# Linear attention and two MLPs in one kernel: the softmax of k on turned tiles, and a new order of the work

## The chip, the cores and the metric

The kernel runs on one core of a Trainium2 chip. The metric is the device time of one execution in microseconds. Engines are named as the profile names them: PE is TensorE (matmuls), PEld its weight loads, DVE is VectorE, ACT is ScalarE, POOL is GpSimd, SP is SyncE, which here issues the DMAs.

## What is computed

```python
def _attn_ref(q, k, v):                       # q, k, v: 4 x 8 x 576 x 64, float32
    q_s = softmax of q along the 64 features
    k_s = np.exp(k - np.max(k, axis=2, keepdims=True))
    k_s = k_s / (np.sum(k_s, axis=2, keepdims=True) + 1e-09)     # along the 576 tokens
    kv = np.einsum('bhsd,bhse->bhde', k_s, v)
    return np.einsum('bhsd,bhde->bhse', q_s, kv)

x = attn_out, as 2304 tokens x 512
x = softplus(x @ w_in) @ w_out                # 512 -> 2048 -> 512
return elu(x @ w2_in) @ w2_out                # 512 -> 2048 -> 512
```

## The kernel before

The 2304 tokens are six blocks of 384 (t = 0 to 5); two blocks make a pair p. For a pair, each of the two MLPs (m = 0, 1) runs through eight quads f of 256 hidden features. All but the first quad use a seven-product scheme on half blocks: the sums that it needs of x and of the weights are formed on ACT and DVE, each as a high and a low part that TensorE multiplies as fp32r. The products are `ub`, `ua`, `uc` (up, line 975) and `acc`, `Pa`, `Pb`, `Pc` (down, lines 1174, 1205, 1347). The first quad (m = p = f = 0) is done directly in fp32: `up` (line 1037) and its `acc` (line 1142).

Before a block of x exists, attention has to be done for it. Heads go in pairs hp = 0 to 3, one head on partitions 0 to 63 and the other on 64 to 127. `add_k` makes the 64 x 64 matrices `kvbd` of a batch b and its head pairs; `add_q` makes x for a block from q and `kvbd`: `pq` (transposes, line 627), `xq` (copy), `px` (line 643), `sx` (copy, line 656). Block 0 needs batch 0, four head pairs one at a time; block 1 needs batches 0 and 1, and batch 1 goes in two calls with two head pairs each. For these two blocks `add_k` has the tokens of a head on 64 partitions, nine to a partition. In `k` the maximum over tokens therefore goes across partitions:

- DVE takes the maximum over the nine (`mt`, `mx`, line 356, four instructions), TensorE transposes it (`pt`, line 364), DVE reduces (`m`, line 368), TensorE spreads the result over the partitions (`pb`, line 376), DVE subtracts it from k (line 383), ACT takes exp (line 391).
- TensorE multiplies by v, to which a column of ones is added (`pk`, line 400: 18 matmuls of 64 x 64 by 65 columns for a head pair, in fp32, with the two heads on different halves of the array). DVE makes the reciprocal of the sums (`rs`, lines 415 and 419), ACT scales into `kvbd` (line 429, two instructions for a head pair).

Later blocks take their k on all 128 partitions (`add_k_wide`); that code is unchanged.

The order of all work comes from a planner in the file (`class Plan`). Each piece is a step with an engine, an estimated duration, what it reads and writes, and which buffer ring it needs. `order()` runs through time and picks on each engine, among steps that can start, the one with the earliest due time; due times run back from those of the `up` and `acc` steps, and the table `PRI` moves groups of steps earlier or later (`k00` is k of block 0 and head pair 0, `i3` the input weights of quad 3). Each engine then executes its list in that order. The set `LIGHT` names weight tiles whose first ACT step (line 791) is done as a `Prelu` while the table of exp is loaded; for those the DVE step in line 804 is left out. Buffers matter in one place: k of batch 1 has a ring of one, so its second call is loaded only after `pk` has read the first.

Of the kernel before, what the change touches and what calls it, by code (L numbers as in the profile page):

```python
# [21 lines left out]
class Plan:  # L22
# [38 lines left out]
    def order(self):  # L61
# [23 lines left out]
        seq, gone = [], set()  # L85
        while len(seq) < n:
# [30 lines left out]
            if eng == PE and t < 25:  # L117
                dur *= PE_EARLY
            if i in gone:
                dur = 0.0  # L120
            if i in self.either and (self.tab[i] or table) == "exp":
                gone.add(self.either[i][0])
                self.light.add(self.either[i][1])
# [26 lines left out]
PE_EARLY = 1.6  # L150
# [7 lines left out]
def t_dve(n, fast=False):  # L158
    return 0.069 + n / (1920 if fast else 960)
# [11 lines left out]
def attention_moe_moe_kernel(  # L171
# [34 lines left out]
    P = 128  # L206
# [87 lines left out]
    def bank(t, rows=False):  # L294

        return "ha" if t > 1 else "acc0" if rows and not t else "acc1"

    def add_k(t, b, hps, behind=()):
# [52 lines left out]
        mt = ("mt", b, hps[0])  # L351

        @step(DVE, sum(t_dve(n * x * D) for x in (4, 2, 1, 1)) + 0.37, r=[kk], make=[(mx, "mx"), (mt, "mt")])
        def _():
            half = new(mt)[:, : 4 * n * D].rearrange("p (g c d) -> p g c d", g=n, d=D)
            top = lambda o, x, y: nc.vector.tensor_tensor(o, x, y, op=ALU.max)
            top(half, kt()[:, :, :4], kt()[:, :, 4:8])
            top(half[:, :, :2], half[:, :, :2], half[:, :, 2:])
            top(half[:, :, 0], half[:, :, 0], half[:, :, 1])
            top(new(mx)[:, : n * D].rearrange("p (g d) -> p g d", g=n), half[:, :, 0], kt()[:, :, 8])  # L360

        @step(PE, 0.11, r=[mx], make=[(pt, bank(t))])
        def _():
            nc.tensor.transpose(new(pt)[: n * D, :P], T[mx][:, : n * D], ident)

        @step(DVE, t_dve(128), r=[pt], make=[(m, "m")])
        def _():
            nc.vector.tensor_reduce(
                new(m)[: n * D], T[pt][: n * D, :P].rearrange("d (h p) -> d h p", h=2), axis=AX.X, op=ALU.max
            )  # L370

        @step(PE, 0.12 * n, r=[m], make=[(pb, bank(t))])
        def _():
            p = new(pb)
            for j in range(2):
                nc.tensor.matmul(
                    p[64 * j : 64 * j + 64, : n * D], T[m][: n * D, j : j + 1].to_broadcast([n * D, 64]),
                    ident[: n * D, : n * D], start=True, stop=True,
                )

        @step(DVE, t_dve(n * C * D), r=[pb], w=[kk])
        def _():
            nc.vector.tensor_tensor(
                kt(), kt(),
                T[pb][:, : n * D].rearrange("p (g o d) -> p g o d", g=n, o=1).to_broadcast([P, n, C, D]),
                op=ALU.subtract,
            )

        @step(ACT, t_act(n * C * D), w=[kk], tab="exp")
        def _():  # L390
            nc.scalar.activation(kt(), kt(), AF.Exp)

        @step(PE, 1.3 * n, r=[kk, vk], make=[(pk, bank(t))])
        def _():
            p = new(pk)
            for g in range(n):
                for c in range(C):
                    for j in range(2):
                        rows = slice(64 * j, 64 * j + 64)
# [7 lines left out]
    def add_kv(b, hps):  # L407
# [13 lines left out]
        eng = ACT  # L421

        @step(eng, 0.65 * n, r=[pk, rs], w=[("kvbd", b % 2, hp) for hp in hps])
        def _():
            for g, hp in enumerate(hps):
                for j in range(2):
                    rows = slice(64 * j, 64 * j + 64)
                    o, i, f = kvbd[b % 2, hp][rows, rows], pkv()[rows, g, :D], T[rs][rows, g : g + 1]
                    nc.scalar.activation(o, i, AF.Copy, scale=f)
# [273 lines left out]
    def add_forms(m, p):  # L703
# [50 lines left out]
        (0, "i", 0), (0, "i", 2), (0, "i", 3), (0, "i", 4), (0, "i", 5), (0, "o", 0), (0, "o", 6), (0, "o", 7),  # L754
        (1, "i", 4), (1, "o", 1), (1, "o", 6), (1, "o", 7),
# [996 lines left out]
```

## Time and profile before

| | |
|---|---|
| median of 3 runs | 817.21 us (816.12 to 818.25) |
| the profiled execution | 817.89 us |
| its span | 815.8 us |
| PE busy | 796.9 us, 98% of the span |
| DVE, ACT busy | 655.2 us, 581.5 us |
| HBM | 154.66 MB read, 56.10 MB written |

The profiled execution is 0.7 us above the median. All windows and start times below count from the start of the span. A matmul in plain fp32 leaves two records in the trace, one in fp32r and a transpose leave one. A duration is that of a record or of a merged run of records; since matmuls are pipelined, the time that a run of them takes is read from its start to the start of what follows.

### The profile page before, as it was taken

The page shows a single profiled execution, that of the slowest core. Times are in us where ns is not written, and L with a number is a line of the kernel's source. Part 1 is how long each engine was busy: PE and PEld are TensorE (multiplying, and loading weights), DVE is VectorE, ACT ScalarE, POOL GpSimd, SP SyncE. Part 2 cuts the span into 40 slices and gives each one's busy share as a digit, 9 for nine tenths or more (in the row PEclk, how much of TensorE's full clock was granted, in tenths as well). Part 3 has the DMA queues.
Part 4 walks back from the last instruction along what each step waited for, and adds up shares of the span by engine and source line. Part 5 has one row for each costly group of instructions (what it writes and reads, how often), then busy time and mean ns, then how long its engine had stood idle before and what let it go on. Part 6 is the DMA issues. An engine that isn't in the chain of part 4 may idle for free.

```text
span 815.8 us, 13597 instructions
## 1 busy us (share of the span) xinstructions
PE 796.9 (98%) x5200; PEld 746.6 (92%) x5200; DVE 655.2 (80%) x1061; ACT 581.5 (71%) x909; POOL 6.9 (1%) x28
## 2 busy tenths in 40 slices
PE   5799999999999999999999999999999999999998
PEld 4578999989899999999999988999999999999998
DVE  7899989989888959987599875579776798767775
ACT  4899898977778879767658765486656675557552
POOL 2000000000000000000000000000000000000000
PEclk9799999999999999999999999999999999999999
DMA  9767797457988557888955889876688767687563
GB/s 284 207 216 224 277 293 223 174 188 270 270 266 301 191 203 271 275 300 290 319 209 215 329 326 358 293 257 261 246 320 297 299 248 252 264 282 301 198 246 134
DMA packets 84993, 211.66 MB, mean 259 GB/s; under 512 B 16064, under 2 KB 51392, under 8 KB 74432
## 3 DMA queue, kind: packets, MB, share of 16 engines
q1 hardware_dynamic: 84928, 210.79, 74.3%
q8 instruction: 41, 0.67, 0.3%
q14 instruction: 24, 0.20, 0.1%
HBM read 154.66 MB, written 56.10 MB: 258 GB/s over the span
## 4 chain that ended last, share of the span: by engine, by line
PE 88%; DMA 4%; ACT 4%; DVE 3%; issue 1%; SPq 0%; ACTq 0%; DVEq 0%
PE acc L1174 23%; PE ub L975 23%; PE uc L975 11%; PE Pb L1347 10%; PE ua L975 6%; PE Pc L1347 5%; PE Pa L1347 3%; PE acc L1205 2%; PE px L643 2%; DMA wos<-wv 1%; DMA q<-in_q_dram 1%; PE pq L627 1%; PE pk L535 1%; DMA wos<-wk 1%; DMA raw_i<-in_moe_w_in_dram 1%
## 5 line engine op out<-in xcount | busy, mean ns | idle before, releaser
L975 PE MATMUL ub<-xf,wf_i 128*128 128x384 f32 x1128 | 229.3, 337 | 1.2 <-ACT s L988 1.2
L975 PEld LDWEIGHTS ub<-xf,wf_i 128*128 128x128 f32 x1128 | 191.4, 188 | 8.5 <-ACT s L988 2.2
L1174 PE MATMUL acc<-gh,wo_o 128*128 128x512 f32 x736 | 160.8, 340 | 0.0
L1174 PEld LDWEIGHTS acc<-gh,wo_o 128*128 128x128 f32 x736 | 118.7, 188 | 11.5
L975 PE MATMUL uc<-xf,wf_i 128*128 128x384 f32 x564 | 114.2, 336 | 0.3 <-DVE xf L728 0.2
L988 ACT COPY s<-ub 128x384 f32<-128x384 f32 x141 | 67.0, 475 | 60.9 <-PE ub L975 59.8
L975 PEld LDWEIGHTS uc<-xf,wf_i 128*128 128x128 f32 x564 | 96.2, 188 | 3.2 <-ACT g L1058 0.5
L1174 PE MATMUL acc<-gl,wo_o 128*128 128x512 f32 x368 | 94.0, 336 | 0.0
L1009 DVE TENSOR_TENSOR h<-uc,s 128x384 f32<-128x384 f32 x94 | 52.1, 554 | 40.2 <-PE uc L975 33.0
L1174 PEld LDWEIGHTS acc<-gl,wo_o 128*128 128x128 f32 x368 | 56.3, 188 | 7.7
L1115 DVE TENSOR_TENSOR gl<-g,gh 128x768 fp32r<-128x768 f32 x54 | 51.4, 953 | 10.5 <-ACT gh L1111 10.3
L975 PE MATMUL ua<-xf,wf_i 128*128 128x384 f32 x282 | 57.2, 337 | 0.0
L975 PEld LDWEIGHTS ua<-xf,wf_i 128*128 128x128 f32 x282 | 48.5, 188 | 1.1 <-DVE h L1009 0.3
L1111 ACT CAST gh<-g 128x768 fp32r<-128x768 f32 x54 | 45.2, 837 | 5.3 <-DVE g L1102 4.5
L1058 ACT ACTIVATE g<-h 128x384 f32<-128x384 f32 (+1 forms) x46 | 31.5, 686 | 7.7 <-DVE h L1009 7.6
L1009 DVE TENSOR_TENSOR h<-ua,s 128x384 f32<-128x384 f32 x47 | 26.0, 553 | 5.9 <-PE ua L975 4.8
L994 ACT COPY h<-ub 128x384 f32<-128x384 f32 x24 | 11.5, 479 | 26.0 <-PE ub L975 25.6
L1205 PE MATMUL acc<-wo_o,gh 128*128 128x512 f32 x96 | 29.9, 392 | 0.0
L890 DVE TENSOR_TENSOR wf_i<-r_i,wf_i 128x1024 fp32r<-128x1024 f32 x20 | 24.4, 1221 | 5.6 <-ACT wf_i L886 5.5
L890 DVE TENSOR_TENSOR wf_i<-st_i,wf_i 128x768 fp32r<-128x768 f32 x27 | 25.6, 950 | 2.0 <-ACT wf_i L886 2.0
L886 ACT CAST wf_i<-r_i 128x1024 fp32r<-128x1024 f32 x20 | 21.0, 1049 | 7.5 <-PE uc L975 5.9
L886 ACT CAST wf_i<-st_i 128x768 fp32r<-128x768 f32 x27 | 22.6, 839 | 4.5 <-DVE st_i L869 4.4
(328 smaller groups left out, 1498.7 us busy)
## 6 DMA issues: line engine op xcount, KB each, us to landing
wf_i<-wfd SPq DMA_DIRECT2D x20, 1792.0 KB, 7.9
ws<-wos SPq DMA_DIRECT2D x35, 1024.0 KB, 6.2
raw_i<-in_moe_w_in_dram SPq DMA_DIRECT2D x32, 512.0 KB, 5.4
raw_o<-in_moe_w_out_dram SPq DMA_DIRECT2D x32, 512.0 KB, 4.7
wo_o<-wod SPq DMA_DIRECT2D x15, 1024.0 KB, 5.5
r_i<-w32i SPq DMA_DIRECT2D x20, 512.0 KB, 4.1
wod<-wo_o SPq DMA_DIRECT2D x8, 1024.0 KB, 5.2
wfd<-wf_i SPq DMA_DIRECT2D x4, 1792.0 KB, 7.1
```

The costliest lines, as they stand in the source:

```text
L643: nc.tensor.matmul(ov[:, :, n0 : n0 + n_], kvbd[b % 2, hp], iv[:, :, n0 : n0 + n_], start=True, stop=True,)
L886: nc.scalar.copy(view(0, lo, n), get())
L890: nc.vector.tensor_tensor(view(1, lo, n), get(), view(0, lo, n).bitcast(F32), op=ALU.subtract)
L975: nc.tensor.matmul(ps[:, :BLK], T[wk][:, lo : lo + P], T[xk][:, (2 * c + kc) * BLK : (2 * c + kc + 1) * BLK], start=(i in first and kc == ...
L988: nc.scalar.copy(new(sk), T[key][:, :BLK])
L1009: nc.vector.tensor_tensor(T[hk][:, half * BLK : (half + 1) * BLK], T[key][:, :BLK], T[sk], op=ALU.add)
L1058: nc.scalar.activation(o, i, AF.Softplus)
L1111: nc.scalar.copy(new(hk), T[gk])
L1115: nc.vector.tensor_tensor(new(lk), T[gk], T[hk].bitcast(F32), op=ALU.subtract)
L1174: nc.tensor.matmul(ps, T[wk][:, lo : lo + P], T[g][:, cols], start=(first and n == 0 and starts), stop=(f == NQ - 1 and j == 1 and n == 2) ...
L1205: nc.tensor.matmul(ps, T[g][:, col : col + P], T[wk][:, (2 * a + j) * DM : (2 * a + j + 1) * DM], start=(first and n == 0), stop=(f == PRE ...
L1347: nc.tensor.matmul(ps[:, x * 256 : x * 256 + 256], T[fk][a][:, r * P : (r + 1) * P], T[ck][:, q * 512 + b * 256 : q * 512 + b * 256 + 256] ...
```

## The change

For blocks 0 and 1 `add_k` turns k of a head pair so that the 64 features of a head stand on partitions and its tokens along the free dimension. Turning is 18 matmuls of 64 x 64 whose moving side is a 64 x 64 identity, in plain fp32, not transposes: `ka`, and `kx` for the last of the nine pieces. DVE reduces the maximum along the free dimension (two instructions and a small one that joins and negates them), ACT takes exp from PSUM with the maximum as its bias (two instructions). The result is turned back in the same way (`ea`, and another slice of `kx`), DVE copies it to `k` in SBUF (two instructions), and `pk` follows as before. `mt`, `mx`, `pt`, `pb` and the subtraction are gone for these blocks. `kx` is one PSUM tile for all head pairs, opened at the start.

`kvbd` of batches 0 and 1 is scaled by DVE instead of ACT. The planner's model of a slow TensorE is another one (a state with a gap and a run in place of "the first 25 us"), `pk` has 1.07 in place of 1.3 us in it and a turning 0.54 us. `LIGHT` has 19 members in place of 12, and `PRI` is new, so that the order changes in all of the first MLP and the start of the second. The last 1305 rows of PE's list are the same.

```diff
-PE_EARLY = 1.6
+PE_EARLY, PE_GAP, PE_RUN = 1.85, 2.0, 4.6
...
+        def turned_to(wide, more, get):
+            for c in range(C):
+                for rows in two:
+                    to = T[wide][rows, c * 64 : c * 64 + 64] if c < C - 1 else T[kx][rows, more * 64 : more * 64 + 64]
+                    nc.tensor.matmul(to, get(rows, c), ident[rows, rows], start=True, stop=True)
...
-        def _():
-            half = new(mt)[:, : 4 * n * D].rearrange("p (g c d) -> p g c d", g=n, d=D)
...
+            @step(PE, 0.54, r=[kk, ("kxr",), *([("kt", 0, hp)] if b else [])], make=[(ka, "ha" if early else "acc1")], w=[k9], hold=[kx])
+                turned_to(ka, hp, lambda rows, c: kt()[rows, g, c, :])
...
+                nc.vector.tensor_reduce(new(m)[:, :1], T[ka], axis=AX.X, op=ALU.max)
+                nc.vector.tensor_reduce(T[m][:, 1:2], last_(0), axis=AX.X, op=ALU.max)
...
+                nc.vector.tensor_scalar(
+                    T[m][:, :1], T[m][:, :1], T[m][:, 1:2], -1.0, op0=ALU.max, op1=ALU.mult
+                )
...
+                nc.scalar.activation(flat()[:, :512], T[ka], AF.Exp, bias=T[m][:, :1])
+                nc.scalar.activation(flat()[:, 512:], last_(0), AF.Exp, bias=T[m][:, :1])
...
+            @step(PE, 0.54, r=[kt_, *([("ke", 0, hp)] if b else [])], make=[(ea, "ha" if early else "acc1")], w=[e9], hold=[kk, kx])
+                turned_to(ea, 4 + hp, lambda rows, c: flat()[rows, c * 64 : c * 64 + 64])
...
+                copy(flat()[:, :512], T[ea])
+                copy(flat()[:, 512:], last_(1))
...
-        @step(PE, 1.3 * n, r=[kk, vk], make=[(pk, bank(t))])
+        @step(PE, 1.07 * n, r=[vk] + [("ke", b, hp) for hp in hps], make=[(pk, bank(t))], hold=[kk])
...
-        eng = ACT
+        eng = DVE if b in (0, 1) else ACT
...
+                        nc.vector.tensor_scalar(o, i, f, None, op0=ALU.mult)
...
-        k00=165, q00=153.5, k01=696.5, q01=214, k02=165.5, q02=417, k03=1898, q03=1032, k10=31.5, q10=133, k12=1338.5,
+        k00=196.5, q00=20, k01=25, q01=221, k02=64, q02=111, k03=94.5, q03=184.5, k10=141, q10=208.5, k12=174, q12=27,
```

The start of PE's list, before (in a name the first number is the batch or block, the second the head pair; `k_1_2` holds head pairs 2 and 3 of batch 1):

```order
L364 MATMUL pt_0_3_205<-ident_147,mx_0_3_200 64x128
L376 MATMUL pb_0_3_218<-ident_147,m_0_3_209 64x64 x2
L364 MATMUL pt_1_2_226<-ident_147,mx_1_2_215 128x128
L376 MATMUL pb_1_2_241<-ident_147,m_1_2_232 64x128 x2
L400 MATMUL pk_0_3_248<-v_0_3_182,k_0_3_183 64x65 x18
L364 MATMUL pt_0_1_284<-ident_147,mx_0_1_239 64x128
L364 MATMUL pt_0_2_291<-ident_147,mx_0_2_278 64x128
L376 MATMUL pb_0_1_298<-ident_147,m_0_1_289 64x64 x2
L400 MATMUL pk_1_2_308<-v_1_2_186,k_1_2_187 64x65 x36
L400 MATMUL pk_0_1_368<-v_0_1_190,k_0_1_191 64x65 x18
```

and now:

```order
L370 MATMUL ka_0_0_198<-ident_147,k_0_0_183 64x64 x16
L370 MATMUL kx_196<-ident_147,k_0_0_183 64x64 x2
L370 MATMUL ka_0_3_229<-ident_147,k_0_3_191 64x64 x16
L370 MATMUL kx_196<-ident_147,k_0_3_191 64x64 x2
L370 MATMUL ea_0_0_250<-ident_147,k_0_0_183 64x64 x16
L370 MATMUL kx_196<-ident_147,k_0_0_183 64x64 x2
L419 MATMUL pk_0_0_283<-v_0_0_182,k_0_0_183 64x65 x18
L370 MATMUL ka_1_3_304<-ident_147,k_1_2_187 64x64 x16
L370 MATMUL kx_196<-ident_147,k_1_2_187 64x64 x2
L370 MATMUL ea_0_3_331<-ident_147,k_0_3_191 64x64 x16
L370 MATMUL kx_196<-ident_147,k_0_3_191 64x64 x2
L370 MATMUL ka_0_2_359<-ident_147,k_0_2_194 64x64 x16
```

Each head pair had one transpose, two spreading matmuls and its `pk`; now it has two turnings of 18 matmuls ahead of `pk`, and head pair 0 of batch 0 is the first.

The place of the first `up` in PE's list, before:

```order
L627 MATMUL pq_0_1_568<-ident_147,q_0_1_272 128x128 x3
L627 MATMUL pq_0_0_573<-ident_147,q_0_0_387 128x128 x3
L376 MATMUL pb_1_0_581<-ident_147,m_1_0_577 64x128 x2
L643 MATMUL px_0_1_587<-xq_0_1_567,kvbd0_1_149 128x384
L643 MATMUL px_0_0_590<-xq_0_0_572,kvbd0_0_148 128x384
L1037 MATMUL up_0_0_0_604<-sx_0_0_179,w_ti_0_i_0_543 128x384 x4
L627 MATMUL pq_1_0_621<-ident_147,qn_1_0_609 128x128 x3
L627 MATMUL pq_1_1_628<-ident_147,qn_1_0_609 128x128 x3
L400 MATMUL pk_1_0_634<-v_1_0_395,k_1_0_396 64x65 x36
L1037 MATMUL up_0_0_1_676<-sx_0_0_179,w_ti_0_i_0_543 128x384 x4
```

and now, from the last `px` of block 0:

```order
L665 MATMUL px_0_0_753<-xq_0_0_740,kvbd0_0_148 128x384
L649 MATMUL pq_1_2_759<-ident_147,qn_1_2_751 128x128 x3
L370 MATMUL ka_1_0_767<-ident_147,k_1_0_691 64x64 x16
L370 MATMUL kx_196<-ident_147,k_1_0_691 64x64 x2
L370 MATMUL ka_1_1_792<-ident_147,k_1_0_691 64x64 x16
L370 MATMUL kx_196<-ident_147,k_1_0_691 64x64 x2
L649 MATMUL pq_1_3_812<-ident_147,qn_1_2_751 128x128 x3
L1060 MATMUL up_0_0_0_824<-sx_0_0_180,w_ti_0_i_0_503 128x384 x4
L370 MATMUL ea_1_0_841<-ident_147,k_1_0_691 64x64 x16
L370 MATMUL kx_196<-ident_147,k_1_0_691 64x64 x2
L665 MATMUL px_1_2_865<-xq_1_2_758,kvbd0_2_150 128x3x64
L665 MATMUL px_1_2_865<-xq_1_2_758,kvbd1_2_154 128x3x64
```

Before, all of block 0 stood ahead of the first `up`, and the `px` of head pairs 3 and 2 of block 1 too. Now the turnings `ka` of batch 1's second call stand ahead of it, and the turnings back and all `px` of block 1 behind it.

In the new list some products also wait for ACT or DVE before they write `kx`. With the waits written out, PE's rows for the second and the fourth turning:

```order
L370 MATMUL ka_0_3_229<-ident_147,k_0_3_191 64x64 [waits DMAHW3_49]
L370 MATMUL ka_0_3_229<-ident_147,k_0_3_191 64x64 x15
L370 MATMUL kx_196<-ident_147,k_0_3_191 64x64 [waits Activation_49]
L370 MATMUL kx_196<-ident_147,k_0_3_191 64x64
L370 MATMUL ea_0_0_250<-ident_147,k_0_0_183 64x64 [waits PE_49]
L370 MATMUL ka_1_3_304<-ident_147,k_1_2_187 64x64 [waits DMAHW2_49]
L370 MATMUL ka_1_3_304<-ident_147,k_1_2_187 64x64 x15
L370 MATMUL kx_196<-ident_147,k_1_2_187 64x64 [waits Activation_49]
```

The last two matmuls of a turning go to the shared tile and have a wait of their own, behind which the rest of PE's list stands.

## Rows read from the trace of the kernel before

**Rows 1.** The page, busy time, share of the span and instructions of each engine.

```profile
PE 796.9 (98%) x5200; PEld 746.6 (92%) x5200; DVE 655.2 (80%) x1061; ACT 581.5 (71%) x909; POOL 6.9 (1%) x28
```

**Rows 2.** Windows: us, busy us (xcount) of PE, PEld, DVE, ACT, POOL; PEclk; DMA share; GB/s.

```profile
15.00:20.00 5.00, 5.00 (x101) 4.93 (x99) 5.00 (x14) 3.52 (x6) 1.62 (x2) 1.00 1.08 361
...
40.00:45.00 5.00, 5.00 (x86) 3.92 (x84) 4.20 (x6) 4.98 (x8) 0.00 (x0) 1.00 0.45 131
...
60.00:70.00 10.00, 9.86 (x51) 8.07 (x50) 9.84 (x17) 9.89 (x13) 0.00 (x0) 1.00 0.64 170
```

**Rows 3.** Waits of PE, whole span: us in total, times, longest us.

```profile
PE pt L364 <- DVE mx L356: 6.5, 2, 5.0
PE px L643 <- ACT xq L633: 1.7, 2, 1.4
...
PE ub L975 <- ACT s L988: 1.2, 2, 0.8
```

**Rows 4.** Timeline of PE: start us, us, what, xrecords, [idle before <-releaser].

```profile
14.29 5.64 PE L400 MATMUL pk<-v,k 64*64 64x65 f32 x108 [0.22 <-issue]
19.87 0.55 PE L627 MATMUL pq<-ident,q 128*128 128x128 f32 x3
21.93 0.27 PE L364 MATMUL pt<-ident,mx 128*64 128x128 f32 x1 [1.51 <-DVE qd L605]
23.56 1.65 PE L643 MATMUL px<-xq,kvbd 128*128 128x384 f32 x2 [1.36 <-ACT xq L633]
...
26.42 0.69 PE L376 MATMUL pb<-ident,m 64*64 64x64 f32 x8
...
36.19 1.56 PE L643 MATMUL px<-xq,kvbd 128*128 128x384 f32 x4 [0.31 <-ACT xq L633]
39.23 2.85 PE L1037 MATMUL up<-sx,w_ti_i 128*128 128x384 f32 x8 [1.49 <-ACT sx L656]
41.92 0.82 PE L627 MATMUL pq<-ident,qn 128*128 128x128 f32 x6
42.67 2.32 PE L400 MATMUL pk<-v,k 64*64 64x65 f32 x72
44.91 2.85 PE L1037 MATMUL up<-sx,w_ti_i 128*128 128x384 f32 x8
47.60 1.46 PE L643 MATMUL px<-xq,kvbd 128*128 128x192 f32 x8
48.90 1.45 PE L1142 MATMUL acc<-g,w_ti_o 128*128 128x384 f32 x4
```

**Rows 5.** Windows of 1 us, PE alone: busy us (xcount), PEclk, DMA share, GB/s.

```profile
31.00:32.00 1.00, 1.00 (x26) 0.50 0.02 7
...
33.00:34.00 1.00, 1.00 (x15) 1.00 0.00 0
```

**Rows 6.** DMA issued between 2.1 and 2.4 us: KB each, us from issue to landing.

```profile
k<-in_k_dram SPq DMA_DIRECT2D x1, 288.0 KB, 4.7
```

**Rows 7.** Timeline of DVE: columns as in rows 4.

```profile
3.57 0.42 DVE L356 TENSOR_TENSOR mt<-k 128x256 f32<-128x256 f32 x1 [3.57 <-DMA k<-in_k_dram]
4.03 0.55 DVE L356 TENSOR_TENSOR mt<-mt 128x128 f32<-128x128 f32 x2
4.61 0.22 DVE L356 TENSOR_TENSOR mx<-mt,k 128x64 f32<-128x64 f32 x1
5.41 0.28 DVE L368 TENSOR_REDUCE m<-pt 64x2 f32<-64x128 f32 x1 [0.58 <-PE pt L364]
...
15.08 0.74 DVE L383 TENSOR_TENSOR k<-k,pb 128x576 f32<-128x576 f32 x1
```

**Rows 8.** Line 1551, a DVE copy of 512 columns from PSUM: ns min/median/max.

```profile
L1551 DVE COPY yt<-acc x9: 677/684/692, 193.8 to 471.9; 128x512 f32<-128x512 f32 x9
```

**Rows 9.** Timeline of ACT: columns as in rows 4.

```profile
13.56 0.63 ACT L429 ACTIVATE kvbd<-pk,rs 64x64 f32<-64x64 f32 x2 [0.35 <-DVE rs L419]
```

**Rows 10.** Line 804, the DVE step that the light form leaves out.

```profile
L804 DVE SCALAR_TENSOR_TENSOR ti_i<-raw_i,ti_i x7: 1218/1226/1227, 131.3 to 356.7; 128x1024 uint32<-128x1024 uint32 x7
```

More of the change, by code (lines that the diff above doesn't have):

```diff
@@ L85, in order @@
         seq, gone = [], set()
+        pe_warm, pe_from, pe_end = False, 0.0, 0.0
         while len(seq) < n:
@@ L116, in order @@
             _, dur, _, _, new, keys, _, after, port, _ = self.steps[i]
-            if eng == PE and t < 25:
-                dur *= PE_EARLY
             if i in gone:
                 dur = 0.0
+            if eng == PE:
+                gap = t - pe_end
+                if gap > (PE_GAP if pe_warm else 0.6):
+                    pe_warm, pe_from = False, t
+                if not pe_warm:
+                    dur *= PE_EARLY
+                pe_end = t + dur
+                pe_warm = pe_warm or pe_end - pe_from >= PE_RUN
             if i in self.either and (self.tab[i] or table) == "exp":
@@ L347, in _ @@
                     nc.sync.dma_start(out=vt()[:, g, :, :D], in_=vsrc(hp))
-        mt = ("mt", b, hps[0])
-        @step(DVE, sum(t_dve(n * x * D) for x in (4, 2, 1, 1)) + 0.37, r=[kk], make=[(mx, "mx"), (mt, "mt")])
-        def _():
-            half = new(mt)[:, : 4 * n * D].rearrange("p (g c d) -> p g c d", g=n, d=D)
[L356 to L369, printed above, removed]
-            )
[L372 to L391, printed above, removed]
-        @step(PE, 1.3 * n, r=[kk, vk], make=[(pk, bank(t))])
+        kx = ("kx",)
@@ new lines, in add_k, with _ @@
+        if not kload.keys() - {(b, hp) for hp in hps}:
+            @step(POOL, 0.0, make=[(kx, "acc0")], w=[("kxr",)], behind=[kload[b, 0]])
+            def _():
+                new(kx)
+        two = [slice(64 * j, 64 * j + 64) for j in range(2)]
+        def turned_to(wide, more, get):
[3 more added lines that the diff above has]
+                    nc.tensor.matmul(to, get(rows, c), ident[rows, rows], start=True, stop=True)
@@ L397, in _ @@
                 for c in range(C):
-                    for j in range(2):
-                        rows = slice(64 * j, 64 * j + 64)
+                    for rows in two:
                         nc.tensor.matmul(
@@ L419, in _ @@
             nc.vector.reciprocal(T[rs][:, :n], T[rs][:, :n])
-        eng = ACT
-        @step(eng, 0.65 * n, r=[pk, rs], w=[("kvbd", b % 2, hp) for hp in hps])
+        eng = DVE if b in (0, 1) else ACT
+        @step(eng, 0.28 * n if eng == DVE else 0.65 * n, r=[pk, rs], w=[("kvbd", b % 2, hp) for hp in hps])
         def _():
@@ L428, in _ @@
                     o, i, f = kvbd[b % 2, hp][rows, rows], pkv()[rows, g, :D], T[rs][rows, g : g + 1]
-                    nc.scalar.activation(o, i, AF.Copy, scale=f)
+                    if eng == DVE:
+                        nc.vector.tensor_scalar(o, i, f, None, op0=ALU.mult)
+                    else:
+                        nc.scalar.activation(o, i, AF.Copy, scale=f)
     def add_k_wide(t, b, hps, behind):
@@ L753, in attention_moe_moe_kernel @@
     LIGHT = {
-        (0, "i", 0), (0, "i", 2), (0, "i", 3), (0, "i", 4), (0, "i", 5), (0, "o", 0), (0, "o", 6), (0, "o", 7),
-        (1, "i", 4), (1, "o", 1), (1, "o", 6), (1, "o", 7),
[3 rows of a table added]
     }
```

26 lines of the change are left out of this document (22 added, 4 removed), and 3 rows, old and new, of the table LIGHT.

## The prediction

> **What bounds the kernel now.** I read the page first: PE is busy 796.9 of 815.8 us, DVE 80% and ACT 71% [rows 1]. So the time is TensorE's work plus what TensorE loses, and the question is where it loses. The view of PE's waits gives nearly all of its idle time to the first 40 us; after 60 us the largest wait is 1.2 us in total, before `ub` [rows 3]. The windows agree: from 40 us PE is full, and it stays full at 60 to 70, although DVE and ACT are full there as well (9.84 and 9.89 of 10 us) [rows 2]. Hence the end is set by the moment at which TensorE has finished the attention of blocks 0 and 1 and the two first `up`, and has only the MLPs in front of it. In the trace that is 48.90, where the first `acc` starts [rows 4]. I follow both lists to the same set of finished PE work, and the difference is the change of the time.
>
> **Prices of PE's pieces**, from starts in PE's timeline [rows 4]. A `pk` of one head pair: 72 records, two head pairs, take from 42.67 to 44.91, so 1.12 us each. At the slow clock, three head pairs take from 14.29 to 19.87, so 1.86 us each. (The granted clock reads 1.00 there [rows 2], but the durations are those of the stretch that reads 0.50 later [rows 5], so I go by the durations: 1.2 GHz there, 2.4 GHz later.) `pq` is 0.75 us for two, 41.92 to 42.67. `px` is 1.30 for two, 47.60 to 48.90. An `up` is 2.69, 44.91 to 47.60.
>
> PE's work up to 48.90 at these fast prices: 8 head pairs of `pk` 9.0, 8 `pq` 3.0, 8 `px` 5.2, two `up` 5.4, and 6 `pt` and 6 `pb` some 2.3 (a `pt` 0.27; two `pb` 0.69 at the slow clock, so 0.17 each, or twice that for the two wide ones). Together 24.9. So TensorE loses 24.0 of its first 48.9 us, by waits and by the slow clock.
>
> **What the change adds to PE.** Eight head pairs are turned there and back: 16 turnings of 18 fp32 matmuls, 64 x 64 by 64 columns, two heads on the two halves. That is `pk` with 64 columns for 65. I take 1.10 us at the fast clock and 1.83 at the slow one. The bounds: from below a transpose, which leaves one record in place of two; three of 128 columns take 0.375 us, so 18 of 64 columns on two halves take 0.56. From above the 1.12 of `pk`. I take the upper one because the program has plain products here, like `pb`, whose two matmuls for a head pair leave four records (x8 for two) [rows 4]. The sum: 16 x 1.10 = 17.6 us more, 2.3 less, so 24.9 + 15.3 = 40.2 us of work to the same point.
>
> **What TensorE would lose then.**
> - Start: the first k lands as before; DVE started on it at 3.57 [rows 7]. 3.6 us, unchanged.
> - The next k to be turned (head pair 3) is the fourth load. The fourth load was issued at 2.1 and took 4.7 us [rows 6], so it is there at 6.8; the first turning ends at 3.6 + 1.83 = 5.4. Lost: 1.4.
> - Turning, turning, turning back end at about 10.5. Then `pk` waits for the copies of DVE: a copy of 512 columns is 0.68 [rows 8], the one of 64 some 0.15, with the way there about 1.0. Lost: 1.0.
> - The slow clock: six units (three turnings, `pk`, two turnings) end at 17.1 if slow, 0.74 lost on each: 4.4. Bounds: four (3.0), since before the change the three slow `pk` of 14.29 to 19.87 came without a gap and the `pq` behind them took 0.55 for three, between slow and fast; and eleven (8.1), if it is as slow as later, where TensorE was busy without a gap from 23.56 and read 0.50 until 32 [rows 4, 5].
> - Waits for DVE and ACT from there on: here I have no row for the new list. The nearest are the waits of the old list between 20 and 40 us: 1.51, 1.36, 0.31 and 1.49, together 4.7 [rows 4]. The new list has places of the same kind: `pk` of head pair 2 behind two copies that stand behind a weight step on DVE, `pk` of the batch-1 pair behind three maxima of q and a subtraction, the last `px` of block 0 behind two weight steps on ACT, and `pq` of head pair 0 of block 1 behind the sums of the last `pk`. I take 4.7, with bounds 0 and 9.4. The new waits before the writes to `kx` are in this: behind them stands all of PE's list, and the readers they wait for are an exp or a reduction of 64 columns that was issued a turning earlier.
>
> Together 3.6 + 1.4 + 1.0 + 4.4 + 4.7 = 15.1. The loss falls from 24.0 to 15.1, because the turnings fill the idle time and keep TensorE at work; but the work grows by 15.3. The same point comes at 40.2 + 15.1 = 55.3 in place of 48.9: **6.4 us later**.
>
> **What costs nothing.** On DVE a head pair loses the chain of `mt` and `mx` (1.19 busy), `m` 0.28 and the subtraction 0.74 [rows 7], and gains a reduction and a copy of 512 columns (0.68 each [rows 8]), their two small ones and the two scalings into `kvbd`, about 2.2 for 2.2. ACT loses 8 x 0.63 of `kvbd` [rows 9]. Seven weight tiles more in light form save DVE 1.23 us each [rows 10], 8.6 in all, for two more table loads on ACT. All of this lies beside a full PE, and where DVE and ACT were full, at 60 to 70, PE lost 0.14 us [rows 2]. If the cover went, some of the 1.2 us that `ub` waits [rows 3] would go or double; I leave it in the range. On SP the first weights, two loads of 0.5 MB, now stand ahead of every q; at the 361 GB/s of 15 to 20 us [rows 2] that delays q by 2.9 us, but its first product on PE comes behind eight units, after 19 us. k of batch 1's second call waits for `pk` of the first as before; between the two stand more than 4 us of PE's work, about what a load takes [rows 6].
>
> The profiled execution took 817.9, so the sum gives 824.3 on it; it stands 0.7 above the median, so I predict 823.6 against the median of 817.2.
>
> **A rule against the change.** In the trace a record of `pk` takes 31 ns (2.24 us for 72), while a record of `px` with 192 columns takes 0.163 us, 0.85 ns a column [rows 4]: 65 columns alone would take 55. So the two halves overlap, though both write one PSUM bank. The Trainium skill, TensorEngine Tiling (Array Packing), Gotcha 1: PSUM Pressure, states that row tiles cannot access the same PSUM bank at the same time. By that rule a turning would take 36 x 54 ns = 1.95 us and the time be about 837; the rows of `pk` speak against it.
>
> **Rivals.**
> - *The turnings cost half, and DVE sets the pace.* At 0.56 the work is 24.9 + 6.7 = 31.6; DVE's chain is no shorter, so the later waits double to 9.4, the first gaps grow by 1, and the slow clock costs 2.7. Loss 3.6 + 1.4 + 1.0 + 1.0 + 2.7 + 9.4 = 19.1: the same point at 50.7, +1.8, 819.0. Chance 0.10.
> - *The turnings cost half and the waits don't grow.* 31.6 + 14.4 = 46.0, so 2.9 sooner: 814.3. This is the side on which the kernel gets faster; it decides below a price of about 0.73 for a turning. For it: the old list left 24 us of TensorE unused. Against: the records of `pb` and `pk`. Chance 0.12.
> - *Right price, no waits behind 17 us*, since the new order was made for these steps: 6.4 - 4.7 = +1.7, 818.9. Against: DVE is as loaded as before. Chance 0.14.
> - *The clock stays slow*, eleven units: +3.7 more, 827.3. Chance 0.12.
> - *The halves take turns* (above): 837. Chance 0.02.
>
> My forecast itself has 0.50, with its own range from 820 to 827.5. A difference of 0.3% is 2.45 us, about what a measurement can tell here: faster is below 814.8, slower above 819.7. So faster 0.12; the same 0.24 (first and third rival); slower 0.64. The range from 816 to 829 takes in the forecast, the two cases of the same and the slow clock, and leaves out the faster case and the halves in turn.
>
> **What would show it.** Right: `ka` and `ea` leave 36 records a head pair and take about 1.1 us when fast and 1.8 when slow; PE's busy time grows by more than 15 us while its idle time before 40 us falls by several; the first `acc` and the `px` of block 1 are through at about 55; from there on the trace runs as before. Wrong: turnings of 0.6 us, or one record for each matmul; a PE that is through with block 1 before 49; a new idle stretch behind 60 us.

## The result

The changed kernel takes 828.6 us (median of six runs, 827.0 to 831.7); the kernel before took 816.7 beside it (816.1 to 818.3). The ratio is 1.0146, 95% interval 1.0125 to 1.0167: slower by about 12 us. A later set (run 11) gave 1.0127 (1.0109 to 1.0144). The forecast was 823.6, with a range up to 829. So the sign and the range held, the range by 0.4 us; the size was too small by 5 us, and the narrower range that the forecast gave for itself, 820 to 827.5, was missed.

The profiled execution took 827.42 us, with a span of 825.4. That is 9.5 above the profiled execution of before, and 1.2 below the median of its own runs, while the one of before stood 1.2 above its median: most of the 11.9 between the medians is in the two traces.

The page of the changed kernel, busy time of each engine:

```profile
PE 808.8 (98%) x5746; PEld 759.2 (92%) x5746; DVE 650.4 (79%) x1074; ACT 583.1 (71%) x905; POOL 6.8 (1%) x28
```

Against [rows 1], TensorE is busy for 11.9 us more, and its idle time falls from 18.9 to 16.6 (span less busy time). The sum, 9.6, is the longer span. DVE and ACT are busy for about as long as before, so neither can explain the difference by its total load.

The windows of both kernels show where TensorE's idle time went; the columns are those of [rows 2]. First the kernel before, then the changed one:

```profile
0.00:40.00 40.00, 26.45 (x283) 20.46 (x284) 31.74 (x81) 27.13 (x47) 6.40 (x24) 0.87 0.87 250
40.00:60.00 20.00, 20.00 (x144) 14.63 (x143) 17.99 (x24) 18.70 (x29) 0.13 (x1) 1.00 0.67 207
```

```profile
0.00:40.00 40.00, 29.13 (x666) 26.06 (x666) 26.54 (x80) 21.60 (x35) 6.26 (x24) 1.00 0.73 227
40.00:60.00 20.00, 19.59 (x270) 14.73 (x269) 17.29 (x34) 16.04 (x25) 0.13 (x1) 1.00 0.61 209
```

In the first 40 us TensorE is busy for 2.7 us more, and the mean granted clock reads 1.00 instead of 0.87: the stretch at 0.50 [rows 5] is gone. That is what the filling of gaps gives back, and it is worth little: executions of the kernel before in which the mean granted clock reads 1.000, so that this stretch is missing there too, take 815.4 us (median of 9 beside the experiments), those at 0.996 or less 817.1 (15 of them).

PE's waits of the changed kernel (us in total, times, longest), beside [rows 3]:

```profile
PE ka L370 <- DMA k<-in_k_dram: 4.9, 2, 3.7
PE pk L419 <- DVE k L411: 2.4, 2, 1.3
PE pq L649 <- DVE q L636: 1.3, 1, 1.3
PE ea L370 <- ACT k L395: 1.2, 1, 1.2
...
PE pk L419 <- POOL v L335: 0.6, 1, 0.6
```

The 6.5 us that `pt` waited are gone with `pt`. In their place stand the waits of the first two turnings for their loads and the waits of `pk` for the copies that bring the turned exps back.

PE's timeline of the changed kernel, columns as in [rows 4]:

```profile
3.67 1.97 PE L370 MATMUL ka<-ident,k 64*64 64x64 f32 x32 [3.67 <-DMA k<-in_k_dram]
5.40 0.45 PE L370 MATMUL kx<-ident,k 64*64 64x64 f32 x4
7.09 1.97 PE L370 MATMUL ka<-ident,k 64*64 64x64 f32 x32 [1.24 <-DMA k<-in_k_dram]
...
9.06 1.92 PE L370 MATMUL ea<-ident,k 64*64 64x64 f32 x32
...
12.53 2.21 PE L419 MATMUL pk<-v,k 64*64 64x65 f32 x36 [1.34 <-DVE k L411]
14.51 1.59 PE L370 MATMUL ka<-ident,k 64*64 64x64 f32 x32
...
16.04 1.11 PE L370 MATMUL ea<-ident,k 64*64 64x64 f32 x32
...
17.09 1.11 PE L370 MATMUL ka<-ident,k 64*64 64x64 f32 x32
...
23.05 1.15 PE L370 MATMUL ka<-ident,k 64*64 64x64 f32 x32
...
24.25 0.91 PE L665 MATMUL px<-xq,kvbd 128*128 128x384 f32 x2
25.00 0.49 PE L649 MATMUL pq<-ident,q 128*128 128x128 f32 x3
...
28.82 1.27 PE L419 MATMUL pk<-v,k 64*64 64x65 f32 x36 [1.08 <-DVE k L411]
...
57.08 1.46 PE L1165 MATMUL acc<-g,w_ti_o 128*128 128x384 f32 x4
58.37 1.46 PE L665 MATMUL px<-xq,kvbd 128*128 128x192 f32 x8
59.54 1.36 PE L998 MATMUL ub<-xf,wf_i 128*128 128x384 f32 x6
```

A turning is the 32 records of `ka` (or `ea`) and the 4 of `kx`: 36 records, from 7.09 to 9.06 at the slow clock (1.97 us) and from 16.04 to 17.09 at the fast one (1.05). The change in pace is near 15 us, in the fourth turning. The slow pace is read from these durations, as in the prediction; the column of the granted clock reads 1.00 there as well. The last `px` of block 1 is through at 59.54; two `acc` (57.08 to 58.37) that stood behind it before are done by then, so the point that the prediction followed, 48.90 before [rows 4], is at 59.54 - 1.29 = 58.25. It is 9.35 later, and from there to the end of the span it is 767.2 us against 766.9: nearly the whole difference lies in the first 60 us.

### The profile page after: what moved, and what is told of

The parts are those of the page before. It is cut to its first block, busy times and chain, and to the rows that moved or that the text cites. A ratio compares the mean times of both kernels' runs of the same rounds, so it can differ in the third digit from the quotient of the medians.

```text
span 825.4 us, 14696 instructions
## 1 busy us (share of the span) xinstructions
PE 808.8 (98%) x5746; PEld 759.2 (92%) x5746; DVE 650.4 (79%) x1074; ACT 583.1 (71%) x905; POOL 6.8 (1%) x28
## 4 chain that ended last, share of the span: by engine, by line
PE 90%; DMA 4%; DVE 4%; ACT 2%; issue 0%; SPq 0%; DVEq 0%; ACTq 0%
PE ub L998 23%; PE acc L1197 22%; PE uc L998 11%; PE Pb L1370 10%; PE ua L998 6%; PE Pc L1370 5%; PE Pa L1370 3%; PE acc L1228 2%; DMA wos<-wk 2%; PE px L665 2%; DMA q<-in_q_dram 1%; PE up L1060 1%; PE pq L649 1%; PE ka L370 1%; PE pk L557 1%; PE acc L1165 1%
## 5 line engine op out<-in xcount | busy, mean ns | idle before, releaser
L1197 PEld LDWEIGHTS acc<-gh,wo_o 128*128 128x128 f32 x736 | 118.8, 188 | 11.9
```

What stands on the lines that cost most here:

```text
L1197: nc.tensor.matmul(ps, T[wk][:, lo : lo + P], T[g][:, cols], start=(first and n == 0 and starts), stop=(f == NQ - 1 and j == 1 and n == 2) ...
```

## The experiments

All ratios are to the kernel before, timed on the same chip.

**1. Every first turning done twice.** The theory under test was the prediction's: the time is TensorE's work. The rival was that the new order loses it by waits.

```diff
             for rows in two:
                 to = T[wide][rows, c * 64 : c * 64 + 64] if c < C - 1 else T[kx][rows, more * 64 : more * 64 + 64]
                 nc.tensor.matmul(to, get(rows, c), ident[rows, rows], start=True, stop=True)
+                if more < 4:
+                    nc.tensor.matmul(to, get(rows, c), ident[rows, rows], start=True, stop=True)
```

> The changed kernel with every turning there (ka and its part of kx) done twice, one after the other into the same place; the planner is not told, so each engine's list is the same but for the doubled products. Work theory (the time goes by TensorE's work up to the first acc, and a turning costs its own 1.05 us, 1.97 at the slow clock): eight turnings more, two or three of them slow, so 9 to 11 us more than the changed kernel, 838 to 840. Order theory (the loss comes from the new order and its chains of waits, in which the turnings lie hidden): under 3 us more, 829 to 832.

Measured: 837.2 us, ratio 1.0261 (1.0243 to 1.0278), 9.4 above the changed kernel by the ratios, some 2 us either way by their intervals. The page:

```profile
PE 816.9 (98%) x6034; PEld 767.5 (92%) x6034; DVE 650.4 (78%) x1074; ACT 582.6 (70%) x905; POOL 6.8 (1%) x28
```

The span is 834.9, 9.5 more than the changed kernel's: 8.1 of it is busy time and 1.4 idle. A doubled turning takes 2.10 us where it runs fast (13.18 to 15.28), so eight extra ones are 8.4. The waits moved too: the one for the second load is gone (1.2), and a pause of 2.1 us stands in the sixth turning, for which the profile shows no releaser. So extra work on TensorE arrives about in full. That says that TensorE has no slack in the new list; it doesn't yet say that less work would be returned.

**2. One half turned by transposes**, to halve the price of a turning.

```diff
-                    nc.tensor.matmul(to, get(rows, c), ident[rows, rows], start=True, stop=True)
+                    nc.tensor.transpose(to, get(rows, c), ident[rows, rows]) if not rows.start else nc.tensor.matmul(to, get(rows, c), ident[rows, rows], start=True, stop=True)
```

> The changed kernel with the first head's half of every turning done as transposes, one record in place of two: 27 records a turning in place of 36. Same lists otherwise. Work theory: a turning takes 0.79 in place of 1.05 us, 16 x 0.26 = 4.2 us less, 824.4. Order theory: within 1 us of 828.6. If the two halves only overlap while both are products, a turning gets no shorter and nothing can be said.

Measured: 898.9 us, ratio 1.1026 (1.0994 to 1.1059). Its PE timeline:

```profile
3.80 5.17 PE L370 MATMUL ka<-ident,k 64*64 64x64 f32 x24 [3.80 <-DMA k<-in_k_dram]
8.90 0.71 PE L370 MATMUL kx<-ident,k 64*64 64x64 f32 x3
9.54 5.19 PE L370 MATMUL ka<-ident,k 64*64 64x64 f32 x24
```

A turning leaves 27 records in place of 36, as it should, but takes 5.74 us in place of 1.97. Fewer records, and nearly three times the time: this says nothing on the two theories, but it puts the lower bound of the prediction, the price of a transpose on two halves, out of reach for this form.

**3. The changed steps under the old list numbers.**

```diff
     LIGHT = {
-        (0, "i", 0), (0, "i", 1), (0, "i", 2), (0, "i", 4), (0, "i", 7), (0, "o", 1), (0, "o", 2), (0, "o", 3),
...
+        (0, "i", 0), (0, "i", 2), (0, "i", 3), (0, "i", 4), (0, "i", 5), (0, "o", 0), (0, "o", 6), (0, "o", 7),
...
     PRI = dict(
-        k00=196.5, q00=20, k01=25, q01=221, k02=64, q02=111, k03=94.5, q03=184.5, k10=141, q10=208.5, k12=174, q12=27,
...
+        k00=165, q00=153.5, k01=696.5, q01=214, k02=165.5, q02=417, k03=1898, q03=1032, k10=31.5, q10=133, k12=1338.5,
...
```

> The changed kernel with the table PRI and the set LIGHT of the kernel before; turnings, kvbd on DVE and the planner's clock model stay. Work theory: the work of TensorE is that of the changed kernel, so the time stays above 825, and more waits may come on top (up to 835), since the old numbers were not made for these steps. Order theory: most of the loss goes, 817 to 821.

Measured: 889.7 us, ratio 1.0904 (1.0881 to 1.0927); neither theory had that. One wait alone takes a quarter of what it loses against the kernel before:

```profile
PE pq L649 <- DVE qd L622: 18.3, 1, 18.3
```

**4. The old steps under the new list numbers** and the new planner's clock model (the edit of run 3 the other way round in the kernel before, and):

```diff
...
-PE_EARLY = 1.6
+PE_EARLY, PE_GAP, PE_RUN = 1.85, 2.0, 4.6
...
-        @step(PE, 1.3 * n, r=[kk, vk], make=[(pk, bank(t))])
+        @step(PE, 1.07 * n, r=[kk, vk], make=[(pk, bank(t))])
```

> The kernel before (softmax of k by mt, mx, pt, pb and a subtraction, kvbd on ACT) with the changed kernel's PRI, LIGHT and clock model in the planner. Work theory: TensorE's work is that of before, so 815 to 820. Order theory: the loss stays, 825 to 830.

Measured: 829.7 us, ratio 1.0177 (1.0142 to 1.0212). The number is what the rival forecast, but the loss is of another kind than the changed kernel's: TensorE is busy for 799.2 of 826.5 us, so it is idle for 27.3, where the changed kernel is idle for 16.6 and the one before for 18.9. PE's waits are those of the old steps in a worse order.

```profile
PE pt L371 <- DVE mx L363: 6.6, 2, 5.1
PE pk L407 <- issue: 5.8, 4, 2.8
```

In 3 and 4, list numbers did not fit steps for which they weren't found. So these two runs can't tell what the order does apart from the steps, and a part of this change can't be undone by a new run of the planner; from here on, all but one of the experiments keep a list as it is and change only what its steps issue.

**5. The same columns without turning**, by four wide matmuls in place of 18.

```diff
-            for c in range(C):
-                for rows in two:
-                    to = T[wide][rows, c * 64 : c * 64 + 64] if c < C - 1 else T[kx][rows, more * 64 : more * 64 + 64]
-                    nc.tensor.matmul(to, get(rows, c), ident[rows, rows], start=True, stop=True)
+            for rows in two:
+                nc.tensor.matmul(T[wide][rows, :512], ident[rows, rows], get(rows)[:, :512], start=True, stop=True)
+            for rows in two:
+                nc.tensor.matmul(
+                    T[kx][rows, more * 64 : more * 64 + 64], ident[rows, rows], get(rows)[:, 512:], start=True, stop=True
+                )
...
```

> The changed kernel with its list unchanged, but each of the 16 turnings passes k through TensorE without turning it: two matmuls of 512 columns and two of 64 in place of 18 of 64 (left out: the turning itself, so the softmax runs over another axis). By the 0.85 ns a column of `px` in the trace of before, 576 columns take 0.49 us if the halves overlap, about half of the 1.05 measured for a turning. Work theory (the added time is the turnings' own work on TensorE): 16 x 0.56 = 9.0 us less, of which up to 3 come back as waits for DVE and ACT: 819.5 to 823. Rival (the chain through DVE and ACT sets the pace of the new list, the first rival of the prediction): TensorE waits where it worked, 825 to 829. The prediction's second rival (half the price makes the kernel faster than before) would show here as under 814.5. If the halves do not overlap with such wide matmuls, a turning takes 0.98 and nothing is told: 827 to 829.

Measured: 826.5 us, ratio 1.0124 (1.0103 to 1.0146). PE's timeline:

```profile
13.65 1.06 PE L368 MATMUL ka<-k,ident 64*64 64x512 f32 x4
14.51 0.31 PE L370 MATMUL kx<-k,ident 64*64 64x64 f32 x4
14.63 1.06 PE L368 MATMUL ea<-k,ident 64*64 64x512 f32 x4
```

The pass takes 0.98 us, not 0.49: the expectation took 0.85 ns a column from one record of `px`, but an fp32 matmul leaves two records, so a column is 1.70 ns. So the run can't tell the theories apart, although 826.5 lies in the rival's range: the work that was to be halved is still there. What it does tell: 576 columns x 1.70 ns = 0.98 us is the price of the columns of one half alone, so the two halves do run beside each other (one after the other they would take 1.96), and 18 small matmuls (1.05) cost hardly more than 4 wide ones.

**6 and 12. `kvbd` of blocks 0 and 1 back on ScalarE**, in the changed kernel's list:

```diff
-                    if eng == DVE:
+                    if False:
                         nc.vector.tensor_scalar(o, i, f, None, op0=ALU.mult)
                     else:
                         nc.scalar.activation(o, i, AF.Copy, scale=f)
```

> The changed kernel with its list unchanged, but the scalings into `kvbd` of blocks 0 and 1 issued on ScalarE as before the change (two of 0.3 us a head pair there). Work theory: TensorE is behind its own list, the place of the scalings matters only where `px` waits for them: 828 to 831. Rival (DVE is the engine that is late, since `pk` waits 2.4 us for its copies): DVE is relieved, 825 to 828.

Measured: 831.0 us, ratio 1.0186 (1.0158 to 1.0213), which overlaps with that of the changed kernel. So it was run again (run 12) beside the changed kernel (run 11):

> The changed kernel itself, beside the next run on the same chip, so that two medians a few us apart can be compared: 827.5 to 829.5 by the runs so far.

> The changed kernel with `kvbd` of blocks 0 and 1 scaled by ScalarE, again, beside the changed kernel on the same chip. Its first run stood 2.4 us above the changed kernel's median with overlapping intervals; its trace shows a new wait of 2.2 us of `px` for ScalarE's `kvbd`. If that wait is what it costs: 829.5 to 832. If DVE's scalings were free to move: within 1 us of the changed kernel.

Measured: 832.0 us, ratio 1.0176 (1.0157 to 1.0195), against 827.8 us, 1.0127 (1.0109 to 1.0144), for the changed kernel on the same chip. So 4.0 us slower, by the ratios. The new wait in the first of its traces, and what follows it:

```profile
41.41 2.93 PE L665 MATMUL px<-xq,kvbd 128*128 128x384 f32 x4 [2.16 <-ACT kvbd L451]
44.14 0.85 PE L649 MATMUL pq<-ident,qn 128*128 128x128 f32 x3
```

The wait is about half of it: 2.2 more here, 0.7 less at the `pq` before. The rest is pace: behind the wait the granted clock reads 0.50 until about 47 us, and `px`, `pq` and the next two turnings take 6.9 us (41.41 to 48.30) where they take 4.3 in the changed kernel (39.46 to 43.76).

**7. No maximum of k at all**, in the list of before: the bodies of `mt` and `mx`, `pt`, `m`, `pb` and the subtraction are emptied in blocks 0 and 1. It bounds what any other form of that path could bring in this list.

```diff
...
-            nc.tensor.transpose(new(pt)[: n * D, :P], T[mx][:, : n * D], ident)
+            pass
...
-            nc.vector.tensor_tensor(
-                kt(), kt(),
-                T[pb][:, : n * D].rearrange("p (g o d) -> p g o d", g=n, o=1).to_broadcast([P, n, C, D]),
-                op=ALU.subtract,
-            )
+            pass
```

> The kernel before with its list unchanged, but in blocks 0 and 1 the whole path of k's maximum is emptied: the maxima, `pt`, `m`, `pb` and the subtraction (left out: the maximum is not subtracted before the exp). It is what any other form of that path could at most bring. Work theory: TensorE loses the 6.5 us that it waits for `pt` and 2.3 us of `pt` and `pb`, and what is late next is k's exp on ScalarE; 809 to 813. Rival (the first 40 us are bound by loads and by ScalarE, so that the waits only move on to `pk` and `px`): 814 to 817.

Measured: 816.6 us (median of ten), ratio 1.0010 (1.0000 to 1.0019): nothing gained. The wait did move on. PE's waits; then PE's timeline and ACT's, each followed by a row of the kernel before:

```profile
PE pk L384 <- ACT v L342: 9.1, 1, 9.1
PE px L627 <- ACT xq L617: 5.2, 3, 3.7
```

```profile
9.07 2.21 PE L384 MATMUL pk<-v,k 64*64 64x65 f32 x36 [9.07 <-ACT v L342]
...
36.33 2.85 PE L1021 MATMUL up<-sx,w_ti_i 128*128 128x384 f32 x8 [1.49 <-ACT sx L640]
```

```profile
9.71 2.22 PE L400 MATMUL pk<-v,k 64*64 64x65 f32 x36 [0.43 <-issue]
```

```profile
3.59 0.68 ACT L375 ACTIVATE k<-k 128x576 f32<-128x576 f32 x1 [1.58 <-DMA k<-in_k_dram]
8.30 0.67 ACT L342 COPY v<-vr 128x576 f32<-128x576 f32 x1 [4.03 <-DMA vr<-in_v_dram]
...
20.72 1.10 ACT L775 ACTIVATE raw_i<-raw_i 128x1024 f32<-128x1024 f32 x1 [0.60 <-DMA raw_i<-in_moe_w_in_dram]
```

```profile
8.37 0.68 ACT L391 ACTIVATE k<-k 128x576 f32<-128x576 f32 x1 [6.36 <-DVE k L383]
```

The first exp is issued at 3.59 where it was 8.37 before, yet the first `pk` starts at 9.07 where it was 9.71: it needs v, which ACT can copy only when its load has landed, at 8.3. The first `px` waits 3.7 for `xq`, which in ACT's list stands behind the first weight step, and that step waits for its load until 20.72 (it started at 21.87 before). And the first `up` waits 1.49 for `sx` from ACT, as before [rows 4], with ACT busy for 9.89 of the 10 us before 40. So the 6.5 us of `pt` in [rows 3] were one of several parallel paths; the others, the loads of v and of the first weights and then ScalarE's row of copies and exps, were hardly shorter. The trace of before could have shown it: up to 25 us the chain of work that ended last holds one subtraction (0.66 us) of the maximum's path and no `mt`, `mx`, `pt` or `pb`; its longest piece there is the load of q, which landed at 14.12 (start us, us, what):

```profile
5.78 8.34 DMA q<-in_q_dram
```

One caution on these rows: the profiled execution of this run, 814.9 us, is the fastest of its ten, and the one of before, 817.9, is above its median. Its granted clock reads 0.50 for 3 us where that of before does for 10. So the first `up` at 36.33, where it was 39.23, is not a gain that the medians show.

**8. The planner told the right price of a turning** (a new order follows).

```diff
-            @step(PE, 0.54, r=[kk, ("kxr",), *([("kt", 0, hp)] if b else [])], make=[(ka, "ha" if early else "acc1")], w=[k9], hold=[kx])
+            @step(PE, 1.05, r=[kk, ("kxr",), *([("kt", 0, hp)] if b else [])], make=[(ka, "ha" if early else "acc1")], w=[k9], hold=[kx])
...
-            @step(PE, 0.54, r=[kt_, *([("ke", 0, hp)] if b else [])], make=[(ea, "ha" if early else "acc1")], w=[e9], hold=[kk, kx])
+            @step(PE, 1.05, r=[kt_, *([("ke", 0, hp)] if b else [])], make=[(ea, "ha" if early else "acc1")], w=[e9], hold=[kk, kx])
```

> The changed kernel with one number of its planner changed: a turning is costed at 1.05 us, as measured, in place of 0.54. The program then works out the whole order anew. Work theory: the same matmuls have to be done, so it can win at most part of the 7.6 us of waits, and the other numbers of the list were found together with 0.54: 826 to 840. Rival (the loss is the planner's, who counted the turnings at half): 818 to 824.

Measured: 866.5 us, ratio 1.0618 (1.0600 to 1.0637); a miss for both. With one price put right, the other numbers no longer fit: `ub` waits 11.1 us once for a weight step on ACT.

**9. Turnings at a quarter of the price**: k, the exps and the identity are read as bfloat16, the upper half of each word.

```diff
-                    nc.tensor.matmul(to, get(rows, c), ident[rows, rows], start=True, stop=True)
+                    nc.tensor.matmul(
+                        to, get(rows, c).bitcast(mybir.dt.bfloat16)[:, 1::2],
+                        ident[rows, rows].bitcast(mybir.dt.bfloat16)[:, 1::2], start=True, stop=True,
+                    )
```

> The changed kernel with its list unchanged, but the 16 turnings read k, the exps and the identity as bfloat16 (the upper half of each fp32 word, so the lower bits of k and of the exps are left out). The run before with wide matmuls measured 0.98 a turning, since its 576 columns a half cost the same 1.7 ns each however they are cut; with two-byte operands I expect one record for a matmul in place of two and 0.25 to 0.55 us a turning. Work theory: 8 to 13 us less work, of which up to 4 come back as waits for DVE and ACT: 816 to 823. Rival (DVE and ACT set the pace of the new list): the idle time of TensorE grows by what its work falls, 824 to 828. The prediction's second rival, that turnings at half price make the kernel faster than before, would show as under 814.5.

Measured: 822.5 us, ratio 1.0070 (1.0053 to 1.0087). Its page, its timeline and its waits of PE:

```profile
PE 796.9 (97%) x5458; PEld 747.0 (91%) x5458; DVE 650.0 (79%) x1074; ACT 582.8 (71%) x905; POOL 6.8 (1%) x28
```

```profile
12.11 0.64 PE L370 MATMUL ea<-ident,k 64*64 64x64 bf16 x16
...
12.59 0.64 PE L370 MATMUL ka<-ident,k 64*64 64x64 bf16 x16
...
38.02 0.44 PE L370 MATMUL ka<-ident,k 64*64 64x64 bf16 x16
...
38.33 0.42 PE L370 MATMUL ka<-ident,k 64*64 64x64 bf16 x16
...
53.99 1.34 PE L1001 MATMUL ub<-xf,wf_i 128*128 128x384 f32 x6
```

```profile
PE ka L370 <- DMA k<-in_k_dram: 6.4, 2, 3.6
PE pk L422 <- DVE k L414: 3.0, 2, 1.7
PE pb L530 <- DVE m L522: 1.8, 1, 1.8
PE pq L652 <- ACT raw_i L838: 1.7, 1, 1.7
```

A turning is 18 records now, 0.48 us slow (12.11 to 12.59) and 0.31 fast (38.02 to 38.33). From one start to the next, less the idle time between them, the 16 turnings take 8.4 us; in the changed kernel they take 21.8. So 13.4 us of work are gone, and of these 5.6 arrive at the followed point (53.99 - 1.30 = 52.69, against 58.25). The other 7.8 are in the trace: the gaps of TensorE before that point sum to 17.7 us where they were 11.3 (6.4 back), and `pk`, `pq` and `px` from 17.90 to 22.36 are slow again, behind more idle time than before (1.4 back). Behind that point another 1.1 us are lost, where a `pb` waits 1.8 us instead of 0.2, so the spans differ by 4.5. The page says it shortest: TensorE is busy for exactly as long as in the kernel before, 796.9 us, and the span is 5.1 longer, all of it idle. So the time lies in the range of the work theory, but its mechanism holds for less than half: it allowed up to 4 us to come back, and in the main it was as the rival had it, idle time that grows as the work falls.

**10. `kvbd` by VectorE alone**, in the list of before.

```diff
-                    nc.scalar.activation(o, i, AF.Copy, scale=f)
+                    if b in (0, 1):
+                        nc.vector.tensor_scalar(o, i, f, None, op0=ALU.mult)
+                    else:
+                        nc.scalar.activation(o, i, AF.Copy, scale=f)
```

> The kernel before with its list unchanged, but the scalings into `kvbd` of blocks 0 and 1 issued on VectorE, the one part of the change that takes work from ScalarE in the first 60 us. Work theory (TensorE full from 40 us, and before that it waits for the maximum's path on DVE): 815 to 818.5. Rival, after the run without the maximum left the time where it was and showed TensorE waiting for ScalarE (`xq`, `sx`): ScalarE's chain sets the first 40 us, and 5 us less of it give 812 to 815.

Measured: 819.1 us, ratio 1.0033 (1.0021 to 1.0045), 2.7 slower; just outside the first expectation and against the second. `pt` and `pk` now wait for the scalings on DVE:

```profile
PE pt L364 <- DVE kvbd L430: 2.6, 1, 2.6
...
PE pk L400 <- DVE kvbd L430: 1.4, 1, 1.4
```

With 6 and 12: the same sixteen instructions, two for a head pair, cost 2.7 us when moved to DVE in the old list, and 4.0 when moved to ACT in the new one. So neither engine is the right one as such: each list was worse with the other one. No run here was faster than the kernel before.

## Why the prediction came out as it did

The terms of its sum, against the changed kernel's trace up to the same point (us). The waits are read from the rows; the slow clock is what the slow pieces take above the same pieces later; the work is what is left:

| term | predicted | measured |
|---|---|---|
| start, the first k | 3.6 | 3.67 |
| k of head pair 3 | 1.4 | 1.24 |
| first `pk` waits for the copies | 1.0 | 1.34 |
| slow clock | 4.4 | 4.0 |
| later waits | 4.7 | 5.0 |
| work at the fast clock | 40.2 | 43.0 |
| the same point | 55.3 | 58.25 |

- **Where the end is set: right for this change.** The trace from the followed point on is as long as before (767.2 and 766.9), and extra turnings arrive about in full (run 1). The other way round it holds for less than half: of 13.4 us less work, 5.6 arrive there (run 9).
- **The price of a turning: the choice was right**, products and not transposes: 36 records, 1.05 fast and 1.97 slow for 1.10 and 1.83. The rule of the Trainium skill (TensorEngine Tiling (Array Packing), Gotcha 1: PSUM Pressure) would have given 1.95 at the fast clock (the prediction's estimate), for two row tiles that write one bank; neither the 1.05 here nor the 0.98 of run 5 shows that. These tiles differ in rows and columns both, and write different partitions of the bank.
- **The losses: right in sum**, 15.1 predicted and 15.3 measured, in part by luck. The slow clock hit three turnings, one `pk` and part of a fourth turning: those four take 7.8 us where four later ones take 4.7, and the `pk` 0.9 more than its fast price. The later waits are 1.21 (`ea` for the exp), 0.60 (`pk` for v), 1.08, 0.23 and 0.18 (`pk`, the copies), 1.33 (`pq` for q) and 0.40 (`pq`, the sums), 5.03 together. Two of the places that the prediction named are among them, the copies at 28.82 and the sums at 56.40; the wait of the last `px` for weight steps did not come, and those for v, the exp and q were not named. So the size, taken from the old list's gaps, was better than the reasons for it: that is luck.
- **The term that was mis-sized is "PE's work up to 48.90 at these fast prices"** and the turnings priced like it: 40.2 us, measured 43.0. The prices came from runs of equal pieces: two `pk`, two `pq`, two `px` back to back. In the new list the pieces alternate. The last twelve turnings take 14.0 us from start to start, less waits: 1.165 each. The four of them with another turning right behind them take 1.05 to 1.10, the eight with another kind of piece or a wait behind them 1.15 to 1.26. A `px` of block 0 between other pieces is 0.75 (24.25 to 25.00), where 0.65 was taken; a single `pq` 0.39 to 0.55, where 0.375 was taken. By kind: turnings 18.6 (predicted 17.6), `pk` 9.3 (9.0), `pq` 3.5 (3.0), `px` 6.1 (5.2), `up` 5.45 (5.4). That is 2.8 of the 2.95 us that the followed point is late. That the change of kind is the cause is read from these rows; no run tested it by itself.
- **A slip that changed nothing.** Six `pt` at 0.27 and the `pb` at the prediction's prices are 3.0 us, not 2.3. They are in the work of before and gone afterwards, so the 40.2 stays.
- **What remains of the 5.0 us** between 823.6 and 828.6: the sum made 824.3 of the profiled execution, which came out at 827.4, 3.1 more (2.95 of it the followed point); the changed kernel's median stands 1.2 above its profiled execution; and 0.7 had been taken off because the kernel before stood above its median. 3.1 + 1.2 + 0.7 = 5.0. By its number alone, 828.6 is nearest to the rival *The clock stays slow* (827.3), which did not happen: the slow clock cost 4.0, less than forecast.
- **The rival "half price, waits don't grow" is refuted.** It said that below a price of about 0.73 the kernel becomes faster. At 0.31 to 0.48 (run 9) it is still 0.7% slower, because 7.8 of the 13.4 us that TensorE saves are lost again, 6.4 as waits for k, v, DVE and ACT and 1.4 by a slow stretch. The rival "half price and DVE sets the pace" had the mechanism, and was still too low: 819.0 for a price of 0.56, where run 9 stands at 822.5 for less.
- **"For it: the old list left 24 us of TensorE unused" was weak evidence.** Run 7 shows why: with the whole path of the maximum taken out, `pt` and `pb` included, the kernel is as fast as before. In that list the idle time was not held by the maximum alone, so no new form of the maximum could free it there.
- **What "costs nothing" on DVE and ACT: not shown for `kvbd`.** Which engine scales it is worth 2.7 to 4.0 us, by the list that it stands in (runs 6, 10 and 12). The prediction had booked it under covered work. What it costs on DVE in the new list, no run shows.
- Two of the signs named ahead were wrong. PE's busy time grew by 11.9, not by more than 15, because the slow stretches that vanished counted as busy time too. And the first `acc` and the `px` of block 1 were through at 58.4 and 59.5, not at about 55.

Left open: what order would be best for the new steps. Of the 11.9 us, what the order adds and what the turnings add was not separated: runs 3, 4 and 8 only show that the three orders tried are worse, and run 9 that 13.4 us less work in this order is worth about 6; whether numbers found with the right price of a turning would reach 822 or less was not tried.

## What to carry to other kernels

Before a path is rebuilt, empty it: if the kernel without it (run 7) is no faster, the wait that the profile names ends beside another one, and a replacement that adds work has nothing to win in that order. Price small matmuls from places where they stand alone between other pieces, not from back-to-back runs; here that was 2.8 us over 42 pieces. And where a planner's numbers set the order, test a part of a change with the list held fixed, since every new price or step reorders the whole.

## What was not expected of the hardware

- An fp32 turning by 64 x 64 transposes on one half and products on the other takes 213 ns a record (5.74 us for 27 records) at the start of run 2 and 151 ns (4.08 us) in the one turning at the fast pace, against 55 ns (1.97 us for 36) for products on both halves in the same place of the changed kernel.
- In run 2 TensorE hardly paused and yet worked at the slow pace for most of its first 85 us: a turning takes 5.7 to 5.8 us from the start on, one takes 4.1 (51.71 to 55.79), and behind it they take 5.8 again. The column of the granted clock shows only the last part of this. It reads 1.00 up to 55 us; the window of 60 to 80 us reads 0.50 with PE busy for 18.93 of 20 us:

```profile
60.00:80.00 20.00, 18.93 (x115) 12.63 (x115) 5.83 (x12) 4.91 (x9) 1.65 (x2) 0.50 0.16 53
```

- The columns set the price of fp32 products on two halves, hardly the number of products: 1.70 ns a column for each half in 512-column matmuls (run 5), 1.05 us / 576 = 1.82 in 64-column ones. With two-byte operands there is one record for a matmul in place of two, and 0.31 us / 576 = 0.54 ns a column.
